# Eight one-bank accumulator tiles for the layers, and first scores issued inside the branch

## The chip, the cores and the metric

The kernel runs on one core of a Trainium2 chip. The metric is the device time of one execution in microseconds. Before the change it is 552.09 us, the median of 3 runs (551.27 to 553.7).

## What is computed

The program chains three parts, all in float32.

- Attention: 2 batches of 12 heads, 448 tokens, head width 64. Scores are q·kᵀ/8, capped as 30·tanh(s/30), then softmax, then times v. The heads are laid side by side, which gives x with 896 tokens and 768 columns.
- Layer 1: h = x·w_in (768 by 2048), g = max(h,0) + alpha·min(h,0), y = g·w_out (2048 by 768).
- Layer 2: the same shapes, with g = max(h,0)².

```python
x = attn_out.transpose(0, 2, 1, 3).reshape(B * S, H * D)
h = x @ w_in;  g = np.maximum(h, 0.0) + alpha * np.minimum(h, 0.0);  x = g @ w_out
h = x @ w_in2; r = np.maximum(h, 0.0); out = (r * r) @ w_out2
```

## The kernel before

**Start.** `start` (from line 448) issues the DMAs of the first k and q, eight warm-up matmuls into a pool of its own that is closed at once, and then the first three score products (`self.early`, line 474). After them it works out |cap| and reads it into a register of every engine (line 484). `attention_moe_moe` branches on that value (`tc.If`, line 855 on); `run(True)` is the branch that is taken here. In it SyncE and GpSimd begin with `constants` (alpha) and the loads of k, q and v.

**PSUM.** It has eight banks of 512 floats per partition. `start` makes a pool "ps" that lives to the end of the program: three tiles of two banks, `self.ps[n]` of shape [128, 2, 512]. `banks()` hands them out in turn: score products use both banks of a tile. A second pool in the attention has one two-bank tile, "pv".

**Attention** (`fast_attention`, 0 to 100 us): six steps in an order written out by hand for TensorE, ScalarE and VectorE. ScalarE does tanh and exp, TensorE scores and values. At its end three chains of layer 1 are already made (`up_now`).

**Layers** (`layers`, 100 to 546 us). A float32 product is three float32r matmuls: high·high, high·low, low·high, 448 columns each. So `multiply` (line 206) issues three matmuls for each 128 by 128 block of weights. An "up" stage makes, for each of 16 column blocks f, two chains of 18 matmuls, one per batch b, each into one bank. ScalarE and VectorE take a bank out: in layer 2 ScalarE writes max(h,0) (line 288) and VectorE multiplies it with max(h,0) again out of the bank (line 302); for some of the chains lines 296 and 297 do the same. A "down" stage forms a two by two block product by seven products P1 to P7 in place of eight; three banks at a time accumulate, are copied while they go on accumulating (`keep`, line 357), or are added to (lines 347, 348, 360).

The layers' work is not issued in program order. `Plan.order` simulates the engines with fixed costs and writes down, for each engine, the order in which it begins its operations; the instructions are then issued in just that order. A chain of "up" or "down" gets a bank when its first product is placed: the first of a list of free banks. A bank comes back to the end of that list when its last reader is done. The list begins with the two banks of a pool "hm" (which lie where "pv" was), then the first banks of the three "ps" tiles, then their second banks:

```python
banks = [hm.tile([P, self.S], F32, name=f"hm{n}", padded_shape=[P, 512]) for n in range(2)]
banks += [self.ps[n][:, e, :self.S] for e in range(2) for n in range(3)]
plan.tag("ps", banks)
```

Weights come as 64-bit words in 768 KB loads (`load`, line 231) into two raw buffers, each of which is free for the next load when VectorE has joined its words (line 245). In between lie ScalarE (line 247, for half of the second-stage loads also line 241) and VectorE (lines 249 to 254). Sixteen joined weights can wait. `split` makes high and low parts (lines 271 to 273).

The framework adds the semaphore waits: an instruction waits for the earlier instructions that it finds to touch the same tile.

Of the kernel before, what the change touches and what calls it, by code (L numbers as in the profile page):

```python
# [8 lines left out]
F32 = mybir.dt.float32  # L9
# [6 lines left out]
PSUM = bass.MemoryType.PSUM  # L16

P = 128
# [134 lines left out]
class Net:  # L153
# [294 lines left out]
    def start(self, ctx):  # L448

        nc, D, S = self.nc, self.D, self.S  # L450
        self.const = const = self.pool(ctx, "const", 1)
        self.cap_t = const.tile([P, 1], F32, name="cap_t")
        nc.scalar.dma_start(self.cap_t, self.cap.to_broadcast([P, 1]))
        self.raw = const.tile([P, 2, self.NC, P], I64, name="raw")
        x = const.tile([P, 2, self.B, self.NC, S], F32R, name="x")
        self.xh, self.xl = ([x[:, n, b] for b in range(self.B)] for n in range(2))

        first = self.raw[:, 1].bitcast(F32).rearrange("p n f -> p (n f)")
        k, q = (first[:, n * S:n * S + S] for n in range(2))
        nc.sync.dma_start(k, self.kT[:, 0])  # L460
        nc.sync.dma_start(q, self.qT[:, 0])
        self.kq = {0: (k, q)}
        self.ones = const.tile([P, P // 4], F32, name="ones")
        nc.gpsimd.memset(self.ones, 1.0)
        pool = self.pool(ctx, "ps", 1, space=PSUM)
        self.ps = [pool.tile([P, 2, 512], F32, name=f"ps{n}") for n in range(3)]
        self.nbank = -1
        idle = self.xh[0].rearrange("p c s -> p (c s)").bitcast(mybir.dt.bfloat16)[:, :P + 512]
        nc.gpsimd.memset(idle, 0.0)
        with self.tc.tile_pool(name="warm", bufs=1, space=PSUM) as pool:  # L470
            warm = pool.tile([P, 512], F32, name="warm")
            for _ in range(WARM):
                nc.tensor.matmul(warm, idle[:, :P], idle[:, P:], start=True, stop=True)
        self.early = [self.product(0, c) for c in range(3)]
        size = const.tile([P, 1], F32, name="size")
        nc.vector.tensor_scalar_mul(size, self.cap_t, -1.0)
        nc.vector.tensor_max(size, self.cap_t, size)
        self.guard_t = const.tile([P, 1], F32, name="guard_t")
        nc.scalar.activation(self.guard_t, size, AF.Exp, scale=-1.0)
        self.scale_t = const.tile([P, 1], F32, name="scale_t")  # L480
        nc.vector.reciprocal(self.scale_t, self.cap_t)
        nc.vector.tensor_scalar_mul(self.scale_t, self.scale_t, 1.0 / float(D) ** 0.5)
        nc.vector.tensor_scalar_mul(self.guard_t, self.guard_t, 1e-9)
        return nc.values_load(size.bitcast(I32)[0:1, :], skip_runtime_bounds_check_because="it is only compared")
# [275 lines left out]
    def run(self, fast):  # L760
        self.raws = []
        with ExitStack() as ctx:
            wp = self.pool(ctx, "wp", 1)
            splits = {t: [wp.tile([P, self.NC, P], F32R, name=f"{t}{n}") for n in range(SLOTS[t])] for t in ("wh", "wl")}
            self.wh, self.wl = splits["wh"], splits["wl"]
            self.early_g = [wp.tile([P, self.S], F32, name=f"early{f}") for f in range(AHEAD)]
            self.early_t = wp.tile([P, self.S], F32, name="t")
            self.constants()
            region = ExitStack()
            with ExitStack() as actx:  # L770
                self.ap = self.pool(actx, "ap", 2)
                self.early_w = [self.ap.tile([P, self.NC, P], F32, tag="ww", name="ww", bufs=AHEAD) for _ in range(AHEAD)]
                self.dp = self.pool(actx, "dp", 2, space=bass.MemoryType.DRAM)
                self.mm = self.pool(actx, "mm", 1, space=PSUM)
                if fast:
                    region = ctx.enter_context(ExitStack())
                    engines = {mybir.EngineType.PE, mybir.EngineType.Activation, mybir.EngineType.DVE}
                    region.enter_context(self.tc.manual_schedule(engines=engines))
                    self.fast_attention()
                else:  # L780
                    self.general_attention()
                    for f in range(AHEAD):
                        self.fetch(f)
                        self.advance(f, range(6))
                        self.up_now(f)
            lp = self.pool(ctx, "lp", 1, reuse_waits="tile")
            hm = self.pool(ctx, "hm", 1, space=PSUM, reuse_waits="tile")
            self.plan = plan = Plan()
            plan.tag("raw", [self.raw[:, (AHEAD + n) % 2] for n in range(2)])
            plan.tag("w", [lp.tile([P, self.NC, P], F32, name=f"w{n}") for n in range(SLOTS["w"])])  # L790
            for t in ("wh", "wl"):
                plan.tag(t, splits[t][AHEAD:])
            plan.tag("t", [self.early_t])
            plan.tag("g", [lp.tile([P, self.S], F32, name=f"g{n}") for n in range(SLOTS["g"])])
            for t in ("xh", "xl"):
                plan.tag(t, [lp.tile([P, self.S], F32R, name=f"{t}{n}") for n in range(SLOTS[t])])
            banks = [hm.tile([P, self.S], F32, name=f"hm{n}", padded_shape=[P, 512]) for n in range(2)]
            banks += [self.ps[n][:, e, :self.S] for e in range(2) for n in range(3)]
            plan.tag("ps", banks)
            self.layers()  # L800


# [62 lines left out]
```

## Time and profile before

| | us |
|---|---|
| median of 3 runs | 552.09 |
| the profiled execution, whole | 555.1 |
| its span, first to last instruction | 553.2 |
| attention | 0 to about 100 |
| layer 1 up, down | 100 to 208, 208 to 302 |
| layer 2 up, down | 317.6 to 441, 441 to 546 |

| engine | busy us | share of the span |
|---|---|---|
| TensorE matmuls | 531.8 | 96% |
| VectorE | 455.3 | 82% |
| ScalarE | 342.9 | 62% |

The profile is of one execution. TensorE's weight loads have a row of their own (PEld); a load runs beside the matmul before it. "Idle" is the time that an engine stood before an instruction, with the instruction that ended the wait. The trace gives a tile's name without its number, so "ps" is any of the six banks of the three pair tiles and "hm" any of the other two. Matmuls are pipelined and their ends are modelled, so lost time is counted here from start to start.

### The profile page before, as it was taken

To read this page: it belongs to the slowest core of one execution; us is meant where nothing else is said; L and a number is where in the kernel's file an instruction comes from. 1 tells how busy PE (TensorE), PEld (TensorE's weight loads), DVE (VectorE), ACT (ScalarE), POOL (GpSimd) and SP (SyncE) were. 2 spreads that over 40 slices of the span, in tenths; PEclk is the share of its full clock that TensorE was granted. 3 is DMA by queue.
4 is the path that set the end of the run, shared out by engine and by line. 5 is a ranking of instruction groups with operands and counts; after the bars stand their busy time and mean duration, and the time that the engine had idled before them with its cause. 6 is when DMAs were issued, how large, how long until landed. Compare 5 with 4: busy or idle time off the path is not lost.

```text
span 553.2 us, 7040 instructions
## 1 busy us (share of the span) xinstructions
PE 531.8 (96%) x2604; PEld 429.5 (78%) x2604; DVE 455.3 (82%) x639; ACT 342.9 (62%) x468; POOL 23.1 (4%) x36
## 2 busy tenths in 40 slices
PE   7889999999999999999999999999999999999995
PEld 2223345989898998798898887889788898999994
DVE  1799999698789889999998987869788799976661
ACT  6999992455567768956666543446655575455550
POOL 1000000000000000052000000000000000600000
PEclk9999999999999999999999999999999999999999
DMA  6445532145544555597003445645535400930111
GB/s 195 186 164 186 149 121 58 57 140 199 176 124 162 171 172 170 173 224 137 0 2 114 148 139 171 187 156 172 172 114 172 152 20 6 199 96 1 51 50 56
DMA packets 23034, 71.07 MB, mean 128 GB/s; under 512 B 4304, under 2 KB 13008, under 8 KB 22992
## 3 DMA queue, kind: packets, MB, share of 16 engines
q1 hardware_dynamic: 19392, 63.72, 35.3%
q0 software_dynamic: 3456, 6.82, 6.8%
q8 instruction: 22, 0.36, 0.3%
q14 instruction: 20, 0.16, 0.1%
q10 hardware_dynamic: 144, 0.00, 0.0%
HBM read 60.89 MB, written 2.79 MB: 115 GB/s over the span
## 4 chain that ended last, share of the span: by engine, by line
PE 41%; DVE 5%; ACT 3%; issue 1%; DMA 1%; DVEq 0%; ACTq 0%
PE ps L206 31%; PE hm L206 10%; DVE g L302 1%; ACT raw L241 1%; DMA raw<-in_w 1%; DVE w L245 1%; ACT w L247 1%; DVE raw L254 0%; ACT g L288 0%; DVE xl L273 0%; ACT wh L271 0%; DVE g L360 0%; DVE wl L272 0%; DVE raw L252 0%; DVE wl L273 0%
## 5 line engine op out<-in xcount | busy, mean ns | idle before, releaser
L206 PE MATMUL ps<-x,wh 128*128 128x448 f32 x576 | 166.9, 370 | 4.8 <-DVE g L302 2.4
L206 PEld LDWEIGHTS ps<-x,wh 128*128 128x128 f32 x576 | 106.0, 188 | 23.5 <-DVE g L302 6.1
L206 PE MATMUL ps<-x,wl 128*128 128x448 f32 x288 | 105.0, 365 | 0.5 <-DVE wl L273 0.5
L206 PE MATMUL ps<-xh,wh 128*128 128x448 f32 x256 | 94.9, 371 | 2.5 <-ACT g L357 1.4
L206 PE MATMUL ps<-xl,wh 128*128 128x448 f32 x256 | 94.1, 367 | 0.7 <-DVE xl L273 0.6
L206 PE MATMUL ps<-xh,wl 128*128 128x448 f32 x256 | 93.8, 367 | 0.0
L271 ACT CAST xh<-g 128x448 fp32r<-128x448 f32 x90 | 51.0, 568 | 56.6 <-PE ps L206 41.9
L271 ACT CAST wh<-w 128x768 fp32r<-128x768 f32 x77 | 64.5, 837 | 29.7 <-PE ps L206 20.7
L273 DVE TENSOR_TENSOR wl<-w,wh 128x768 fp32r<-128x768 f32 x77 | 73.3, 952 | 10.3 <-ACT wh L271 9.2
L273 DVE TENSOR_TENSOR xl<-g,xh 128x448 fp32r<-128x448 f32 x90 | 55.2, 618 | 15.5 <-ACT xh L271 15.2
L245 DVE SCALAR_TENSOR_TENSOR w<-w,raw 128x768 int32<-128x768 int32 x61 | 58.1, 954 | 11.9 <-ACT raw L241 11.3
L247 ACT ACTIVATE w<-raw 128x768 f32<-128x768 f32 x61 | 55.7, 913 | 18.2 <-DMA raw<-in_w 17.9
L206 PEld LDWEIGHTS ps<-x,wl 128*128 128x128 f32 x288 | 54.0, 187 | 5.3 <-DVE wl L273 0.9
L206 PEld LDWEIGHTS ps<-xh,wh 128*128 128x128 f32 x256 | 48.1, 188 | 10.5 <-ACT g L357 3.4
L206 PE MATMUL hm<-x,wh 128*128 128x448 f32 x192 | 54.5, 365 | 0.0
L206 PEld LDWEIGHTS ps<-xl,wh 128*128 128x128 f32 x256 | 48.1, 188 | 5.7 <-DVE xl L273 1.6
L206 PEld LDWEIGHTS ps<-xh,wl 128*128 128x128 f32 x256 | 48.1, 188 | 4.3
L254 DVE SCALAR_TENSOR_TENSOR raw<-raw 128x768 int32<-128x768 int32 x45 | 42.9, 956 | 1.0
L518 ACT ACTIVATE E<-ps,scale_t 128x896 f32<-128x896 f32 x42 | 40.2, 1025 | 3.3 <-PE ps L503 3.0
L206 PEld LDWEIGHTS hm<-x,wh 128*128 128x128 f32 x192 | 36.0, 187 | 2.9
L523 ACT ACTIVATE E<-E,cap_t 128x1792 f32<-128x1792 f32 (+1 forms) x24 | 38.2, 1623 | 0.0
L503 PE MATMUL ps<-q,k 64*128 64x448 f32 x132 | 30.4, 570 | 5.3 <-ACT E L518 3.0
(105 smaller groups left out, 672.9 us busy)
## 6 DMA issues: line engine op xcount, KB each, us to landing
raw<-in_w SPq DMA_DIRECT2D x64, 768.0 KB, 4.2
g<-g POOLq DMA_DIRECT2D x16, 224.0 KB, 5.2
w<-w POOLq DMA_DIRECT2D x8, 384.0 KB, 6.2
out_T<-g SPq DMA_DIRECT2D x12, 224.0 KB, 2.0
k<-in_kT SPq DMA_DIRECT2D x11, 224.0 KB, 5.0
q<-in_qT SPq DMA_DIRECT2D x11, 224.0 KB, 5.2
v<-in_vT SPq DMA_DIRECT2D x6, 384.0 KB, 5.5
rb<-row SPq DMA_DIRECT2D x10, 224.0 KB, 3.8
```

Source lines behind the costliest of these rows:

```text
L206: self.nc.tensor.matmul(ps, a[:, c, :], m, start=first and n == 0 and not more, stop=last and n == 2, skip_group_check=more)
L241: nc.scalar.mul(halves[:, :, :, 1], parts()[1].bitcast(F32), sign * 2.0 ** -60)
L245: nc.vector.scalar_tensor_tensor(bits, bits, 3, parts()[0], op0=ALU.logical_shift_left, op1=ALU.bitwise_or)
L247: plan.op("ACT", self.act(n) + 0.06, lambda: nc.scalar.mul(w.tile, parts()[1].bitcast(F32), 2.0 ** -112), [high, raw], [w])
L254: plan.op("DVE", self.dve(n), lambda: nc.vector.scalar_tensor_tensor(parts()[0], parts()[0], 29, parts()[1], op0=ALU.logical_shift_right, ...
L271: plan.op("ACT", self.act(n), lambda: nc.scalar.mul(h.tile, w.tile, -1.0) if sign < 0 else nc.scalar.copy(h.tile, w.tile), [w], [h])
L273: if sign < 0 else nc.vector.tensor_sub(l.tile, w.tile, h.tile.bitcast(F32)), [w, h], [l], port=True)
L302: plan.op("DVE", self.dve(S) + 0.06, lambda: nc.vector.scalar_tensor_tensor(g.tile, ps.tile, 0.0, g.tile, op0=ALU.max, op1=ALU.mult), [g, ...
L503: nc.tensor.matmul(ps[:, e, :], k[rows, c * P:c * P + P], q[rows], start=True, stop=True)
L518: nc.scalar.activation(es[-1][:, n % 2], ps, AF.Tanh, scale=self.scale_t)
L523: self.nc.scalar.activation(x, x, AF.Exp, scale=self.cap_t)
```

## The change

The "ps" pool moves from `start` into `run`, in the scope that ends with the attention. The first three score products move with it, behind the branch and ahead of `constants`; they are issued only where the fast attention runs. The layers no longer use the halves of the pair tiles: the pool "hm", opened after the attention's pools are closed, now has eight tiles of one bank. They are listed in an order that gives the same banks in the same sequence as before (6 and 7, where "pv" was, then 0, 2, 4, then 1, 3, 5), so `Plan.order` writes the same order of operations on the same banks.

```diff
@@ start
-        pool = self.pool(ctx, "ps", 1, space=PSUM)
-        self.ps = [pool.tile([P, 2, 512], F32, name=f"ps{n}") for n in range(3)]
-        self.nbank = -1
...
-        self.early = [self.product(0, c) for c in range(3)]
@@ run
-            self.constants()
             region = ExitStack()
             with ExitStack() as actx:
+                pool = self.pool(actx, "ps", 1, space=PSUM)
+                self.ps = [pool.tile([P, 2, 512], F32, name=f"ps{n}") for n in range(3)]
+                self.nbank = -1
+                self.early = [self.product(0, c) for c in range(3)] if fast else []
+                self.constants()
                 self.ap = self.pool(actx, "ap", 2)
...
-            banks = [hm.tile([P, self.S], F32, name=f"hm{n}", padded_shape=[P, 512]) for n in range(2)]
-            banks += [self.ps[n][:, e, :self.S] for e in range(2) for n in range(3)]
-            plan.tag("ps", banks)
+            banks = [hm.tile([P, self.S], F32, name=f"hm{n}", padded_shape=[P, 512]) for n in range(8)]
+            plan.tag("ps", [banks[n] for n in (6, 7, 0, 2, 4, 1, 3, 5)])
```

## Rows read from the trace of the kernel before

**Rows 1.** Page, part 1: busy us, share of the span, instructions.

```profile
PE 531.8 (96%) x2604; PEld 429.5 (78%) x2604; DVE 455.3 (82%) x639; ACT 342.9 (62%) x468; POOL 23.1 (4%) x36
```

**Rows 2.** Windows by stage: length, busy us (instructions) per engine, clock, DMA share, GB/s.

```profile
113.00:208.00 95.00, 95.00 (x464) 86.42 (x464) 81.97 (x113) 61.74 (x93) 0.00 (x0) 1.00 0.51 166
208.00:233.00 25.00, 23.66 (x112) 20.00 (x111) 24.97 (x39) 21.87 (x33) 0.00 (x0) 1.00 0.56 169
233.00:300.00 67.00, 66.27 (x321) 59.60 (x320) 64.10 (x100) 42.00 (x68) 10.62 (x12) 1.00 0.44 106
...
317.60:441.00 123.40, 118.67 (x563) 103.97 (x564) 97.97 (x136) 64.37 (x85) 0.00 (x0) 1.00 0.49 159
```

**Rows 3.** Timeline, 325.2 to 329: start, length, instruction, idle before and its end.

```profile
326.15 0.55 ACT L288 ACTIVATE g<-ps 128x448 f32<-128x448 f32 x1
...
326.36 0.36 PE L206 MATMUL ps<-x,wl 128*128 128x448 f32 x1
...
326.75 0.30 PEld L206 LDWEIGHTS ps<-x,wh 128*128 128x128 f32 x2 [0.41 <-ACT g L288]
...
327.27 0.36 PE L206 MATMUL ps<-x,wl 128*128 128x448 f32 x1
...
327.74 0.62 DVE L302 SCALAR_TENSOR_TENSOR g<-ps,g 128x448 f32<-128x448 f32 x1 [0.50 <-PE ps L206]
...
328.42 0.30 PEld L206 LDWEIGHTS ps<-x,wh 128*128 128x128 f32 x2 [0.56 <-DVE g L302]
```

**Rows 4.** Waits of weight loads, 317.6 to 441: total us, times, longest.

```profile
PEld ps L206 <- DVE g L302: 6.1, 10, 1.1
PEld ps L206 <- ACT g L288: 4.8, 8, 1.1
PEld ps L206 <- DVE g L297: 1.1, 2, 0.6
PEld ps L206 <- DVE x L348: 0.5, 1, 0.5
PEld ps L206 <- ACT g L296: 0.4, 1, 0.4
```

**Rows 5.** Windows inside layer 2 up, columns as in rows 2.

```profile
326.00:341.00 15.00, 13.86 (x63) 11.12 (x62) 10.75 (x15) 6.53 (x10) 0.00 (x0) 1.00 0.46 154
341.00:357.00 16.00, 16.00 (x82) 15.01 (x81) 13.94 (x19) 6.22 (x10) 0.00 (x0) 1.00 0.53 160
```

**Rows 6.** Chain that ended last: start, length, what, matmuls in an unbroken run.

```profile
285.87 14.88 PE ps L206 x72
...
352.84 5.40 PE ps L206 x27
```

**Rows 7.** Timeline, 456 to 459.5, columns as in rows 3.

```profile
457.25 0.53 ACT L357 COPY g<-ps 128x448 f32<-128x448 f32 x1 [0.69 <-PE ps L206]
...
458.14 0.54 ACT L357 COPY g<-ps 128x448 f32<-128x448 f32 x1
...
458.73 0.19 PEld L206 LDWEIGHTS ps<-xh,wh 128*128 128x128 f32 x1 [1.29 <-ACT g L357]
```

**Rows 8.** Timeline of the start, 0 to 40, columns as in rows 3.

```profile
5.00 0.44 PEld L503 LDWEIGHTS ps<-raw 64*128 64x128 f32 x4 [0.84 <-issue]
...
5.21 0.33 SPq L489 DMA_DIRECT2D slope_t<-in_alpha  x1
...
6.27 2.80 ACT L518 ACTIVATE E<-ps,scale_t 128x896 f32<-128x896 f32 x3 [1.49 <-PE ps L503]
```

**Rows 9.** Window of the attention's six steps, columns as in rows 2.

```profile
6.20:80.00 73.80, 68.43 (x388) 23.08 (x384) 61.11 (x74) 71.89 (x65) 0.40 (x2) 1.00 0.54 180
```

**Rows 10.** Loads of weights: six issues in a row from 369.38; all from 320 to 440.

```profile
369.38 21.22 SPq L231 DMA_DIRECT2D raw<-in_w  x6
...
raw<-in_w SPq DMA_DIRECT2D x25, 768.0 KB, 4.2
```

**Rows 11.** Page, part 3: code fetches, packets, MB, share of 16 engines' span.

```profile
q8 instruction: 22, 0.36, 0.3%
```

## The prediction

> **What bounds the kernel now.** I read the engine shares first, then one window per stage, then the waits inside the stage with the most unexplained time, and last its timeline. TensorE is busy 96% of the span [rows 1], so the question is what its few idle microseconds wait for. By stages [rows 2]: layer 1 up (113 to 208) has 464 matmuls in 95.00 us, all of them busy. From 208 to 233 VectorE is busy 24.97 of 25.00 us; it is the bound there. From 233 to 300 TensorE leads again. Layer 2 up (317.6 to 441) has 563 matmuls in 123.40 us, 0.219 each, though its work is layer 1 up's and VectorE is busy only 97.97 of 123.40 there. So layer 2 up loses time to waits, not to work.
>
> How much: in unbroken runs a matmul takes 5.40/27 = 0.200 us in this stage and 14.88/72 = 0.207 at 286 us [rows 6]. At 0.200, 563 matmuls are 112.6 us, so 10.8 of the 123.4 are lost. The weight loads' waits name the causes [rows 4]: lines 302, 288, 297 and 296 take a bank out, and they hold TensorE up 23 times, 12.4 us; one more (line 348) is the wait for the layer's input.
>
> The timeline shows the pattern [rows 3]. At 326.15 ScalarE begins to read one chain's bank. TensorE, which is in the middle of the other chain of the same f, stops when it would issue its next product, and goes on at 326.75, 0.05 after ScalarE's end (326.15 + 0.55). VectorE's line 302, which reads the first bank again and could start at 326.70, waits for TensorE's three matmuls and starts at 327.74. Then TensorE waits until line 302 has ended at 328.36 and goes on at 328.42. Neither needs the other's data. Which bank a chain has follows from `Plan.order`'s free list (its order alone, none of its times): in three of four consecutive f of this stage the two chains sit in the two halves of one pair tile, in the fourth in the two "hm" tiles. The windows agree [rows 5]: 326 to 341 has 63 matmuls in 15 us, while 341 to 357, in which the hm chains run, has 82 in 16 us, without a wait. In layer 1 up the two chains sit in two different tiles, and nothing waits [rows 2]. So the framework tracks the pair tile as one thing: a write into one half waits for a read of the other, and a read of the one for a write into the other.
>
> **The change part by part.** I count lost time from start to start. Around 326.75 three matmuls took 327.27 - 326.36 = 0.91 us and not 0.60, beside a weight-load wait of 0.41 [rows 3]: a wait costs its row less 0.10.
>
> (1) Layer 2 up. One tile per bank takes these 23 waits away. By the wait rows 12.4 - 2.3 = 10.1 us, by the count 10.8 less 0.4 for line 348's wait [rows 4], which is real and stays, 10.4. What is late next? With eight banks and two for each of 16 f, a bank comes round every four f, 4 x 123.4 / 16 = 31 us [rows 2], so no true bank wait follows. VectorE needs 97.97 of then 113 us [rows 2], 87%, and it loses its own half of the ping-pong too: 0.50 us of idle before line 302 [rows 3]. The raw loads: 25 are issued from 320 to 440, 4.8 us apart; the densest six came in 21.22 us, 4.24 apart [rows 10], so 25 need at least 106 us, and 120 - 10.4 = 109.6 remain. It fits, with little to spare. The pace is a second unknown: it is 0.200 in this stage and 0.207 in another [rows 6], and it changes after a wait, so without the waits the stage may run at either. At 0.207 throughout, 563 x 0.0067 = 3.8 us come back. Ends: 10.4 and 6.6. I take the middle, 8.5.
>
> (2) Layer 1 down, from 233. 321 matmuls at 0.203 (between the two paces) are 65.2 of 67.00 us: 1.8 lost; at 0.207 it would be 0.6 [rows 2]. The waits there are of the same kind, copies and additions on the other half. I take 1.4; ends 0.6 and 1.8. From 208 to 233 I take nothing: VectorE's idle time there is 0.03 us [rows 2], so TensorE can't gain more.
>
> (3) Layer 2 down. At 458.73 TensorE has waited for the copy of the other half, 458.14 + 0.54 = 458.68; its own bank's copy ended at 457.25 + 0.53 = 457.78 [rows 7]. That wait becomes 0.9 shorter. Ends 0.5, where the weights are late instead, and 0.9.
>
> (4) First scores behind the branch. No other instruction moves on TensorE, and the products issue no DMA. SyncE's first instruction behind the branch is alpha's load at 5.21, and the first score's weight load stood at 5.00 [rows 8]. TensorE has to read the same register, branch and wait for k and q before it issues, so I put its first score at about 5.4, 0.4 later. Ahead of SyncE's 5.21 it can't be: not under 0.2. The upper end is one code fetch more: 22 fetches hold 0.3% of 16 engines' span, 0.003 x 553.2 x 16 / 22 = 1.2 us each [rows 11], together 1.6. Nothing covers it: the first tanh waits for that product (1.49 us, at 6.27) [rows 8], and ScalarE is busy 71.89 of the next 73.80 us [rows 9], so attention ends later by the same amount. Queued behind the first scores on TensorE are the next products, which wait for tanh to empty a pair; constants' DMA and its GpSimd multiplication need nothing of TensorE. For the order that `Plan.order` writes, nothing changes, and so nothing for SyncE's and GpSimd's queues in the layers.
>
> (5) The seam. The new tiles lie over the attention's, so each one's first matmul waits for the last use of what lay there. The last readers of a pair tile there are two of ScalarE's out of `up_now`'s bank, and the layers' first two chains, 36 matmuls or 36 x 0.207 = 7.5 us [rows 6], go into the "pv" banks, as now. Behind them I cost the wait at nothing; if the first chain had to wait for those two reads it would be 2 x 0.55 = 1.1 us (line 288's length, [rows 3]).
>
> Sum: -8.5 - 1.4 - 0.9 + 0.4 = -10.4 us. Of the profiled execution (555.1 us, of which the span is 553.2) that leaves 544.7. The median of the runs is 3.0 lower, so the forecast for it is 552.1 - 10.4 = **541.7 us**. With every end on the good side -1.8 - 10.4 - 0.9 + 0.2 = -12.9, and about 1 us more if layer 2 down keeps the faster pace: 538. With every end on the bad side -0.6 - 6.6 - 0.5 + 1.6 = -6.1: 546.
>
> **The rivals.** *The loads take over in layer 2 up.* Both raw buffers are always in flight, and each load needs VectorE and ScalarE in their fixed order. If a load keeps 4.7 us (now 4.8, at best 4.24 [rows 10]), 25 take 117.5 us and part (1) gives 2.5 in place of 8.5: 547.7 us. For it: VectorE would wait for line 241 where it now waits for TensorE. Against it: much of the present 4.8 is VectorE waiting for TensorE inside a load's chain.
>
> *The waits stay.* If the framework already told the banks of a pair apart and the waits had another cause, only part (4) is left: 552.5 us. Against it: restarts 0.05 us after the read of the other half, again and again, and none where hm is used.
>
> [...]
>
> *The branch costs a fetch.* GpSimd and SyncE start behind the branch without a gap (5.21 [rows 8]), but TensorE's first instruction there is not seen now. A fetch of 1.2 us [rows 11] plus the wait for a transfer to land, 4.2 as for a load [rows 10], would put the first score up to 5 us later: 546.7. [...]
>
> **How the numbers follow.** Forecast (538 to 546) 77%, loads 12%, waits stay 5%, fetch 4%, clock 2%. The range holds the first, and the loads' and the fetch's times: 537.5 to 548. What a measurement of this kernel can tell from no change is about 0.5%, 2.8 us: 549.3 and 554.9 are the bounds. Forecast, loads and fetch lie below, 0.93 together; one in a hundred is left for a mixture that ends within, so faster 0.92, same 0.06, slower 0.02.
>
> **What would show it.** Right: in layer 2 up no weight load waits for lines 288, 296, 297, 302, line 302 starts at once behind line 288, and 563 matmuls take about 114 to 115 us; 458.73's wait is some 0.4 on its row; the first tanh is at about 6.7. Wrong: such waits for a bank still there (waits stay); waits of matmuls for line 273's high and low parts, with VectorE before line 245 waiting for line 241 (loads); a clock under 1 in a stage (clock); a first score past 6 (fetch). It is also wrong if TensorE's waits vanish but the stage's matmuls take 0.207 each: then part (1) was mis-sized by the pace.

## The result, and the profile after

The changed kernel takes 537.06 us (median of 4 runs, 536.3 to 540.72), the kernel before in the same runs 552.89 (4 runs, 551.27 to 554.69): 15.8 us less. The ratio is 0.9729, interval 0.9681 to 0.9777, with a fifth run of 538.62 in it; the two medians alone give 0.9714. Run once more on another occasion it took 537.17 (5 runs), ratio 0.9699 (0.9675 to 0.9724). The forecast was 541.7 with a range down to 537.5. Direction and mechanism were right; the gain was half as large again as forecast, and the median lies 0.4 us below the low end.

The profiled execution is the slowest of the four, 540.72 us; its span is 538.8, 14.4 less than before's 553.2. First the engine shares, as in [rows 1]:

```profile
PE 524.6 (97%) x2604; PEld 432.3 (80%) x2604; DVE 453.2 (84%) x639; ACT 343.5 (64%) x468; POOL 23.0 (4%) x36
```

The instruction counts are those of before. The windows answer to [rows 2] and [rows 5], the last three shifted by what this kernel is ahead there:

```profile
113.00:208.00 95.00, 94.79 (x459) 85.79 (x460) 82.87 (x115) 61.96 (x93) 0.00 (x0) 1.00 0.52 166
208.00:233.00 25.00, 24.75 (x118) 21.44 (x116) 24.48 (x38) 21.00 (x33) 0.00 (x0) 1.00 0.53 162
233.00:300.00 67.00, 66.42 (x328) 61.58 (x329) 65.93 (x104) 44.23 (x72) 10.62 (x12) 1.00 0.44 109
315.30:427.90 112.60, 112.57 (x564) 105.64 (x564) 95.99 (x136) 64.72 (x85) 0.00 (x0) 1.00 0.53 174
323.70:338.70 15.00, 15.00 (x77) 14.08 (x76) 12.88 (x18) 7.64 (x12) 0.00 (x0) 1.00 0.54 170
338.70:354.70 16.00, 16.00 (x82) 15.02 (x81) 13.34 (x18) 6.75 (x11) 0.00 (x0) 1.00 0.61 199
```

Layer 2 up is the change: from its first matmul to the first of the next stage it takes 112.7 us, where before it took 123.5. The stretch that had 63 matmuls in 15 us now has 77; its neighbour, which had no waits before, still has 82 in 16.

The timeline of the same f as in [rows 3] shows what stopped:

```profile
323.85 0.54 ACT L288 ACTIVATE g<-hm 128x448 f32<-128x448 f32 x1
...
324.05 0.36 PE L206 MATMUL hm<-x,wl 128*128 128x448 f32 x1
324.05 0.39 PEld L206 LDWEIGHTS hm<-x,wh 128*128 128x128 f32 x2
324.25 0.56 PE L206 MATMUL hm<-x,wh 128*128 128x448 f32 x2
...
324.85 0.62 DVE L302 SCALAR_TENSOR_TENSOR g<-hm,g 128x448 f32<-128x448 f32 x1
```

TensorE goes on every 0.20 us while ScalarE (line 288) and then VectorE (line 302) read the other chain's bank, and line 302 begins 1.00 us after line 288, not 1.59 as before. What weight loads still wait for in all the layers (100 to 545; total us, times, longest) is short. None of lines 288, 296, 297 and 302 is left of [rows 4]:

```profile
PEld hm L206 <- ACT g L357: 1.2, 3, 0.5
PEld hm L206 <- DVE xl L273: 1.0, 1, 1.0
PEld hm L206 <- DVE wl L273: 0.9, 1, 0.9
PEld hm L206 <- DVE x L348: 0.4, 1, 0.4
```

The chain that ended last has three unbroken runs of matmuls where [rows 6] had many short ones:

```profile
113.21 109.60 PE hm L206 x529
...
233.58 81.74 PE hm L206 x402
315.34 216.92 PE hm L206 x1067
```

Length by count gives means of 0.2072, 0.2033 and 0.2033 us. Start to start, the steady step is 0.207 us in layer 1 up, 0.203 in layer 1 down and 0.200 in layer 2 up. In layer 2 down it is 0.207, then 0.203, and 0.207 again from 445 us on.

The place of [rows 7], now some 14 us earlier:

```profile
444.34 0.36 PE L206 MATMUL hm<-xh,wl 128*128 128x448 f32 x1
444.54 0.36 PE L206 MATMUL hm<-xh,wh 128*128 128x448 f32 x1
444.61 0.53 ACT L357 COPY g<-hm 128x448 f32<-128x448 f32 x1
...
445.19 0.19 PEld L206 LDWEIGHTS hm<-xh,wh 128*128 128x128 f32 x1 [0.25 <-ACT g L357]
```

The product that began at 458.73 begins here at 444.54, 0.20 after the one before and ahead of the copy that it had waited for. The wait of 0.25 us at 445.19 ends behind that copy (444.61 + 0.53); with one-bank tiles it is a wait for the product's own bank.

The start, as in [rows 8]:

```profile
5.21 0.33 SPq L485 DMA_DIRECT2D slope_t<-in_alpha  x1
...
5.52 0.54 PEld L499 LDWEIGHTS ps<-raw 64*128 64x128 f32 x4 [1.35 <-issue]
...
6.43 0.32 PEld L499 LDWEIGHTS ps<-raw 64*128 64x128 f32 x2 [0.37 <-issue]
...
6.92 0.21 PEld L499 LDWEIGHTS ps<-raw 64*128 64x128 f32 x2 [0.17 <-issue]
...
7.21 1.01 ACT L514 ACTIVATE E<-ps,scale_t 128x896 f32<-128x896 f32 x1 [2.42 <-PE ps L499]
```

The first score's weights are loaded 0.52 later than before, the first tanh begins 0.94 later.

**The sum over the profiled pair.** I set the start of each of the 2604 matmuls against that of the same matmul before (positive: later). Behind the first scores +0.9 to +1.0; at 205 us +1.7; at 247 us +0.90; after layer 1 down (305 us) -2.2; before layer 2 up -2.3; after it -13.1; at the product of 458.73 -14.2; at the last matmul -13.6; at the end of the span -14.4. The 0.6 between the last product named and the last matmul is lost to pace: from 445 us on this execution steps by 0.207, where before stepped by 0.203 until 488. Waits between matmuls of the layers (steps of more than 0.22 us from 100 us on, each less the pace around it) sum to 18.3 us before and 2.8 after.

### The profile page after: what moved, and what is told of

Read it like the earlier page. It is cut to its first block, busy times and chain, and to the rows that moved or that the text cites. A ratio compares the mean times of both kernels' runs of the same rounds, so it can differ in the third digit from the quotient of the medians.

```text
span 538.8 us, 7022 instructions
## 1 busy us (share of the span) xinstructions
PE 524.6 (97%) x2604; PEld 432.3 (80%) x2604; DVE 453.2 (84%) x639; ACT 343.5 (64%) x468; POOL 23.0 (4%) x36
## 4 chain that ended last, share of the span: by engine, by line
PE 86%; DVE 5%; ACT 4%; DMA 2%; issue 1%; SPq 0%; POOL 0%; DVEq 0%; ACTq 0%; POOLq 0%
PE hm L206 77%; PE pv L549 3%; PE ps L206 2%; PE ps L499 2%; ACT E L514 2%; ACT E L519 1%; DVE s L535 1%; DMA r<-rows 1%; DMA k<-in_kT 1%; PE warm L470 1%; PE ps L568 0%; PE pv L559 0%; DVE raw L191 0%; DVE ww L193 0%; DVE raw L254 0%
## 5 line engine op out<-in xcount | busy, mean ns | idle before, releaser
L206 PE MATMUL hm<-x,wh 128*128 128x448 f32 x732 | 208.2, 365 | 0.0
L206 PEld LDWEIGHTS hm<-x,wh 128*128 128x128 f32 x732 | 137.1, 187 | 12.1 <-DVE x L348 0.4
L206 PE MATMUL hm<-x,wl 128*128 128x448 f32 x366 | 133.6, 365 | 0.5 <-DVE wl L273 0.5
L206 PE MATMUL hm<-xl,wh 128*128 128x448 f32 x336 | 123.3, 367 | 0.6 <-DVE xl L273 0.6
L206 PE MATMUL hm<-xh,wh 128*128 128x448 f32 x336 | 123.5, 368 | 0.2
L206 PE MATMUL hm<-xh,wl 128*128 128x448 f32 x336 | 123.2, 367 | 0.0
L206 PEld LDWEIGHTS hm<-x,wl 128*128 128x128 f32 x366 | 68.6, 187 | 6.6 <-DVE wl L273 0.9
L206 PEld LDWEIGHTS hm<-xh,wh 128*128 128x128 f32 x336 | 63.1, 188 | 6.8 <-ACT g L357 1.2
L206 PEld LDWEIGHTS hm<-xl,wh 128*128 128x128 f32 x336 | 63.1, 188 | 6.8 <-DVE xl L273 1.0
L206 PEld LDWEIGHTS hm<-xh,wl 128*128 128x128 f32 x336 | 63.1, 188 | 5.7
```

The costliest lines, as they stand in the source:

```text
L206: self.nc.tensor.matmul(ps, a[:, c, :], m, start=first and n == 0 and not more, stop=last and n == 2, skip_group_check=more)
```

## The experiments

**1. The first scores alone.** The kernel before, with only the pool of pairs and the first scores moved behind the branch. The layers keep the halves, and the pool lives to the end.

```diff
@@ start
-        pool = self.pool(ctx, "ps", 1, space=PSUM)
-        self.ps = [pool.tile([P, 2, 512], F32, name=f"ps{n}") for n in range(3)]
-        self.nbank = -1
-        self.early = [self.product(0, c) for c in range(3)]
@@ run
+            pool = self.pool(ctx, "ps", 1, space=PSUM)
+            self.ps = [pool.tile([P, 2, 512], F32, name=f"ps{n}") for n in range(3)]
+            self.nbank = -1
+            self.early = [self.product(0, c) for c in range(3)] if fast else []
```

> The kernel before with one part of the change alone: the pool of the three pair tiles and the first three score products stand in the branch, and the layers still use the halves of the pairs. Theory (the layers' gain comes from the waits between the halves alone, the moved scores cost what the trace after shows): the first tanh starts at 7.2 us instead of 6.27, every later matmul of the attention is 0.95 us later, layer 2 up still takes 123.4 us, the layers' weight loads still wait for lines 288 and 302 some 23 times there, and the time is the one of before plus about 1 us: 553.9 if before is 552.9 (ratio 1.002). Rival (the gain comes from where the scores and the pool stand, not from the tiles): a clear part of the 15.8 us is gained, ratio 0.99 or less.

Measured: 554.28 us against 552.19, ratio 1.0047 (1.0027 to 1.0067). The waits of weight loads in the layers are those of before:

```profile
PEld ps L206 <- DVE g L302: 6.0, 10, 1.1
PEld ps L206 <- ACT g L288: 5.1, 8, 1.1
```

So this part gains nothing and costs 1.5 to 3.7 us by the times, more than the expected 1. Its start, read as above, shows less than was expected: the weights come at 5.53, the first tanh at 6.68 and not at 7.2, 0.41 later than before, and the matmuls of the attention are 0.4 to 0.6 late, not 0.95:

```profile
5.53 0.33 PEld L499 LDWEIGHTS ps<-raw 64*128 64x128 f32 x4 [1.37 <-issue]
...
6.01 0.22 PEld L499 LDWEIGHTS ps<-raw 64*128 64x128 f32 x2 [0.15 <-issue]
...
6.68 1.91 ACT L514 ACTIVATE E<-ps,scale_t 128x896 f32<-128x896 f32 x2 [1.88 <-PE ps L499]
```

**2. Pair tiles in the new pool.** The changed kernel, with six of the eight banks as three tiles of two banks again. Pool, scope and bank order stay.

```diff
-            banks = [hm.tile([P, self.S], F32, name=f"hm{n}", padded_shape=[P, 512]) for n in range(8)]
+            pairs = [hm.tile([P, 2, 512], F32, name=f"hp{n}") for n in range(3)]
+            banks = [t[:, e, :self.S] for t in pairs for e in range(2)]
+            banks += [hm.tile([P, self.S], F32, name=f"hm{n}", padded_shape=[P, 512]) for n in range(2)]
```

> The kernel after, with the layers' banks 0 to 5 made as three tiles of two banks in the layers' own pool, and 6 and 7 as two tiles of one bank; the banks, their list and the order of the operations are the same. Theory (a wait is drawn between the two banks of one tile): the 18.4 us of waits between layer matmuls come back, where after has 2.8, layer 2 up takes 123 us again, and the time is that of before plus the 0.95 us of the later first scores: 553.8 against 552.9 (ratio 1.002). Rival (what matters is that the attention's pool ends and the layers have a pool of their own): the time of after stays, 537 (ratio 0.971).

Measured: 553.68 us, ratio 1.0025 (1.0011 to 1.0038), and the waits are back, now on tile "hp":

```profile
PEld hp L206 <- DVE g L302: 6.1, 10, 1.1
PEld hp L206 <- ACT g L288: 4.2, 8, 0.8
...
PEld hp L206 <- DVE g L297: 1.1, 2, 0.6
```

This is the decisive one. The banks and their order are those of the changed kernel; only what counts as one tile differs. Where the pool ends and where the first scores stand have no part in the gain; what the framework takes as one tile makes all of it.

**3. Four pairs.** As 2, with the last two banks made one pair too.

```diff
-            pairs = [hm.tile([P, 2, 512], F32, name=f"hp{n}") for n in range(3)]
+            pairs = [hm.tile([P, 2, 512], F32, name=f"hp{n}") for n in range(4)]
             banks = [t[:, e, :self.S] for t in pairs for e in range(2)]
-            banks += [hm.tile([P, self.S], F32, name=f"hm{n}", padded_shape=[P, 512]) for n in range(2)]
```

> As three_pairs, but banks 6 and 7 are also the halves of one tile: four tiles of two banks. The suspected cost is doubled at the place that had none. Theory: the first two chains and, in layer 2 up, every fourth f (the one whose two chains had the two hm tiles) now have the waits too, in the layer 1 up stage as well. Laying the order of the operations over the times of after, waits between halves would come to 18.7 us for the three pairs and 28.8 for four, and three pairs lose 15.6 us in truth; so four lose about 24, 8 more than three: about 562 us (ratio 1.016), with the stretch that has no waits in before (341 to 357) now at about 63 to 70 matmuls in 16 us instead of 80. Rival: 537 (ratio 0.971).

Measured: 559.69 us, ratio 1.0134 (1.0116 to 1.0152). One pair more lengthens the kernel by another 6.0 us, and the waits grow with it (line 302 from 10 to 14, line 288 from 8 to 14). The direction is the expected one, the size is not: 6.0 us and not 8, and the stretch that had no waits in before takes 16.8 us for 80 matmuls where it took 16.0, which is 76 in 16 us and not 63 to 70. Of the 7.3 us of new waits 2.2 are in layer 2 up, the rest in the other stages:

```profile
PEld hp L206 <- DVE g L302: 8.1, 14, 1.1
PEld hp L206 <- ACT g L288: 6.0, 14, 0.6
```

**4. Another order of the free list.** The kernel before, its pairs untouched; only the list's first order differs, so that the two chains of one f share a pair less often.

```diff
-            plan.tag("ps", banks)
+            plan.tag("ps", [banks[n] for n in (3, 4, 2, 0, 5, 1, 6, 7)])
```

> The kernel before with nothing but another order in the list of free banks: pair 1 first half, pair 2 first half, pair 0 first half, hm0, pair 0 second half, hm1, pair 1 second half, pair 2 second half. The order of the operations is the same, every tile is as before; only which two chains share a pair differs. Theory: in layer 2 up the two chains of one f no longer sit in one pair, so their waits go, but other chains share pairs now; laid over the times of after, the waits between halves come to 10.6 us where the list of before has 18.7. So some 43% of the 15.6 us are saved: about 546 us (ratio 0.988). Rival (the waits have nothing to do with which chains share a tile): the time of before, 552.9 (ratio 1.000). Rival (one-bank tiles save something else as well, for every chain): no gain here either.

Measured: 546.96 us, ratio 0.9891 (0.9863 to 0.9918). One reordered list gives a third of the gain by the medians, two fifths by the ratios, without a new tile. Layer 2 up has no wait left, and line 302, the longest holder in [rows 4], is gone. The waits on lines 288 and 290 are now in layer 1 up, which waits 7.1 us where it waited 0.3:

```profile
PEld ps L206 <- ACT g L288: 4.5, 8, 0.7
PEld ps L206 <- ACT t L290: 4.2, 9, 0.8
```

Without a wait, layer 2 up still takes 116.3 us here and not 112.7, because it steps by 0.207, as its unbroken runs show:

```profile
342.65 11.16 PE ps L206 x54
```

**The kernels side by side.** Counted as in the sum above, in one profile of each, the waits between layer matmuls come to 2.8 us in the changed kernel, 11.9 with the other list, 18.3 before, 18.2 with three pairs, 19.1 with the first scores alone and 25.5 with four pairs. The median times are 537.1, 547.0, 552.2, 553.7, 554.3 and 559.7 us. Less its waits, each median lies between 533.9 and 535.5.

**5. The changed kernel again, and two edits of its start.** The first is unedited, a measure for the other two.

> The changed kernel once more, as the measure for the two kernels beside it. Its ratio against the kernel before should be 0.973 again (537 us beside 552), and its first tanh should begin 0.3 to 1.0 us after before's 6.27; in four other kernels this start differed by 0.7 us from one profiled execution to the next.

Measured: 537.17 us against 553.32, ratio 0.9699 (0.9675 to 0.9724). Its start:

```profile
5.51 0.45 PEld L499 LDWEIGHTS ps<-raw 64*128 64x128 f32 x4 [1.35 <-issue]
...
6.14 0.21 PEld L499 LDWEIGHTS ps<-raw 64*128 64x128 f32 x2 [0.17 <-issue]
...
6.80 1.91 ACT L514 ACTIVATE E<-ps,scale_t 128x896 f32<-128x896 f32 x2 [2.02 <-PE ps L499]
```

The weights come at 5.51 as in the first profile, the tanh 0.41 earlier than there. So 0.52 of the 0.94 is the branch, and 0.42 differs between executions of the same code.

The second issues the first two products and their tanh ahead of the branch, out of a pool that is closed there. A tile of the constants, "early_all", holds their result, and the attention's pool waits by tile.

```diff
@@ start
+        with self.tc.tile_pool(name="first", bufs=1, space=PSUM) as pool:
+            self.ps = [pool.tile([P, 2, 512], F32, name=f"first{n}") for n in range(2)]
+            self.nbank = -1
...
+            for c in range(2):
+                nc.scalar.activation(self.first[:, c], self.product(0, c), AF.Tanh, scale=self.scale_t)
@@ run
...
-                self.early = [self.product(0, c) for c in range(3)] if fast else []
...
```

> The changed kernel, with the first two score products and their tanh issued ahead of the branch again (in a pool of two pair tiles that is closed there; the other products stay in the branch). Theory: the move behind the branch costs 0.4 to 0.95 us, paid in full because ScalarE is without a gap from the first tanh on. Then the first tanh is back at 6.3 to 6.9 and the time is 0.1 to 0.2% below the changed kernel's: 536 to 536.6 us, which would beat both. Rival: the start is covered somewhere on the way (VectorE's stretch at 208, the loads) or is lost in what differs from one execution to the next: the same time as the changed kernel within 0.1%. A second rival: the first use of the new pool's tiles behind the branch waits for the early tanh, and the second tanh comes later: 0.1 to 0.3% above.

Measured: 537.63 us, ratio 0.971 (0.9684 to 0.9737), not to be told from 537.17. The first weights are loaded early again, at 5.13, but the tanh is at 7.04 and not at the expected 6.3 to 6.9; and near 55 us this profile loses 1.6 us more, where VectorE waits for a transfer and a product for VectorE:

```profile
5.13 0.51 PEld L506 LDWEIGHTS first<-raw 64*128 64x128 f32 x4 [0.96 <-PE warm L470]
...
6.04 0.34 PEld L506 LDWEIGHTS first<-raw 64*128 64x128 f32 x2 [0.41 <-issue]
...
6.79 0.28 PEld L506 LDWEIGHTS first<-raw 64*128 64x128 f32 x2 [0.41 <-issue]
...
54.25 0.23 DVE L592 TENSOR_SCALAR r<-r,guard_t 128x14 f32<-128x14 f32 x1 [1.52 <-DMA r<-rows]
```

The gain expected of it didn't come. That wait is not its own: in the first profile of the changed kernel VectorE waits 0.7 us for the same transfer, in four_pairs 1.0, in the others it doesn't appear.

The third has nine warm-up matmuls for eight, which shortens TensorE's idle time ahead of its first product: the first weight load waits 0.98 us and not 1.35.

```diff
-WARM = 8
+WARM = 9
```

> The changed kernel with nine warm-up matmuls in place of eight, which shortens TensorE's idle time before the branch by one warm-up matmul. In the changed kernel's profile the second matmul of the first product comes 0.87 us after the first, in before's 0.62. If that is the idle gap's doing, it is 0.62 here and the first tanh about 0.25 us earlier (6.9 to 7.0), which the time can hardly show (0.05%). If the gap has nothing to do with it, 0.87 stays and the first tanh is at 7.2 or, should the ninth matmul delay the branch, later.

Measured: 538.14 us, ratio 0.9717 (0.9692 to 0.9742), again not to be told apart. The weight loads stay 0.91 apart (the second half of the expectation), so that much less idle time doesn't make the first product faster:

```profile
5.57 0.53 PEld L499 LDWEIGHTS ps<-raw 64*128 64x128 f32 x4 [0.98 <-issue]
...
6.48 0.27 PEld L499 LDWEIGHTS ps<-raw 64*128 64x128 f32 x2 [0.38 <-issue]
```

The length of the gap alone doesn't decide it either: before and other_list both begin at 5.00 after a wait of 0.84, and their second loads come at 5.63 and 5.91. Here is before's:

```profile
5.63 0.19 PEld L503 LDWEIGHTS ps<-raw 64*128 64x128 f32 x2 [0.19 <-issue]
```

None of the runs points to a version faster than the changed kernel.

## Why the prediction was right, and where its sizes were wrong

The mechanism is shown. Experiment 2 takes the one-bank tiles away and leaves the rest: the waits and the time return. Experiment 3 makes one pair more, experiment 4 changes which chains share a pair: the time follows the waits.

- **Part (1), layer 2 up: forecast 8.5, measured 10.8.** This is the step that failed in size. I had two paces, didn't know which one the stage would have, and took the middle of 6.6 and 10.4. It kept the faster one, 0.200 us from start to start, in all four profiles of the changed kernel and its edits. So the whole count came through. What decides the pace is open: in experiment 4 the same stage, just as free of waits, ran at 0.207 and gained 7.2 us. Two readings were wrong besides. [rows 4] holds 10 + 8 + 2 + 1 = 21 waits for a bank, not 23 (the wait rows then give 10.3 us and not 10.1, which the forecast didn't use). And line 348's 0.4 was not to be taken off: that wait ends at 317.65, where the stage's first counted matmul begins, so the count of 10.8 never held it.

- **What is late next: nothing, as chosen.** VectorE is busy 95.99 of 112.60 us, 85%. The loads, which I feared might hold at 4.7 to 4.8 us each, went faster. VectorE's waits for TensorE at line 302, 7.5 us in this stage before, are gone; that this is what sped the loads up is argued, not shown. The 25 issues now run from 319.7 to 427.1, 107.4/24 = 4.48 us apart:

```profile
L231 SPq DMA_DIRECT2D raw<-in_w x25: 327/328/328, 319.7 to 427.1; - x25
```

- **Part (2), layer 1 down: forecast 1.4, ends 0.6 and 1.8; measured 3.1.** Three pieces, from the matmul starts of before: waits inside the window 1.8; two more at 300.8 and 301.8 us, just behind the window's end at 300, 0.76; and before ran at 0.207 from 269 to 300, now at 0.203, 0.5. I had cut the window at a round number and then let one pace stand for the stage.
- **From 208 to 233: nothing, as forecast.** TensorE goes out of it 0.90 late, though it came in 1.7 late (before had run its last 28 us of layer 1 up at 0.200 per matmul, here it was 0.207): VectorE, busy 24.48 of 25.00 us, sets that stretch.
- **Part (3): forecast 0.9, measured 1.1.** The product of 458.73 now follows the one before without a wait.
- **Part (4), the branch: forecast 0.4, measured 0.52 to the first weights** in the changed kernel, inside 0.2 to 1.6, and not covered, as said. The tanh's 0.94 holds 0.42 that belongs to the execution. The times of experiments 1 and 2 say more (2.1 and 1.5 us at the medians), and nothing in their traces shows the rest. The edit that issues the first products ahead of the branch didn't give it back. What makes up the difference stays open, and since the first tanh of before's own code came at 6.27 and 6.97 in two profiles, no pair of profiles can size it at the tanh.
- **Part (5), the seam: nothing, as forecast.** The matmuls stay 0.9 to 1.1 late through 113 us without a new wait.
- **Not foreseen:** the stretch from the last matmul to the end took 6.48 us before and 5.72 now, but 6.19 when the same kernel ran again; over all profiles it lies between 5.7 and 6.7. I count it as scatter.

With every end on the good side I had 538, and 537.06 is still below it. Part (1) reached its best end in full and a little more (10.4 forecast, 10.8 measured), and part (2)'s end was too tight. These sizes are of one pair of executions, 14.4 us apart, where the medians are 15.8 apart.

**The rivals.** *Loads:* 4.48 us each, refuted, though VectorE's waits for line 241 ahead of line 245 did grow in layer 2 up, 6.8 to 7.8 us, the sign named for this rival. *Waits stay:* refuted by the waits after and by experiment 2. *Clock* (2% in the forecast): in the changed kernel it reads 1.00 in every window from 0 to 532.6 us, through 1067 matmuls in one piece, and its mean over a run is 0.996 to 1.000 in all runs here. What a lower one would cost, no run shows. *Fetch:* refuted by the first weights at 5.52, behind SyncE's first instruction at 5.21 by 0.31; code fetches are 22 with 0.36 MB as before.

## What to carry to other kernels

Where a framework derives waits from tiles, make each tile as large as what one engine writes while another reads, and no larger: two ping-pong accumulators in one tile are not ping-pong. The sign in a profile is an engine that restarts 0.05 us after a read of data that it doesn't need, in some rounds and not in others of the same work. When such waits go, count them from start to start over the whole stage, with the pace of that stage in that execution, and look at who else was waiting on the other side.

## What the runs showed of the hardware

**The layers' matmuls have several steady paces.** The same stage with the same instructions runs for tens of us at 0.200, 0.203 or 0.207 us per matmul of 448 columns, each with its own weight load (2604 of each in a profile). Most changes come at a wait (before goes from 0.207 to 0.200 at 179.9 us, behind a step of 0.31), but not all: in the first profile of the changed kernel the step goes from 0.200 to 0.207 where layer 2 down begins, and to 0.203 near 431 us, with no step over 0.21 us in between. In four profiles of the changed kernel and its two edits, 400 steps of layer 1 up took 82.67 us three times and 80.00 once (nine_warm), and the last 424 steps of layer 2 down took 87.6 once and 85.9 three times. The two rows below are the stretch of layer 2 from the changed kernel's second profile and from nine_warm, and answer to 216.92 above:

```profile
314.48 215.25 PE hm L206 x1067
```

```profile
312.89 215.25 PE hm L206 x1067
```

Layer 1 up's 2.7 and layer 2 down's 1.7 us together are 4.4, about as much as the runs of one kernel differ (536.3 to 540.72). Which pace comes when is open.

**The first product can run at half its later pace while the clock column says 1.00.** Weight loads of score products follow each other 0.37 to 0.38 us apart later on. At the start the step was 0.91, then 0.75, twice the later one, in other_list, whose start is before's own code:

```profile
5.00 0.51 PEld L503 LDWEIGHTS ps<-raw 64*128 64x128 f32 x4 [0.84 <-issue]
...
5.91 0.34 PEld L503 LDWEIGHTS ps<-raw 64*128 64x128 f32 x2 [0.41 <-issue]
...
6.66 0.34 PEld L503 LDWEIGHTS ps<-raw 64*128 64x128 f32 x2 [0.41 <-issue]
...
6.97 1.91 ACT L518 ACTIVATE E<-ps,scale_t 128x896 f32<-128x896 f32 x2 [2.21 <-PE ps L503]
```

Ahead of it TensorE does nothing but its warm-up matmuls, 0.43 us apart for 512 columns; 512 / 0.43 is 1.2 columns per ns, where a layer matmul at 0.200 us passes 448 / 0.200 = 2.2. The step falls to 0.37 at a moment that differs between executions, from about 5.6 us (before) to 7.2 (other_list), and moves the first tanh of one and the same code by up to 0.7 us (6.27 and 6.97). The granted clock reads 1.00 in every window of the start (0 to 8 us, nine profiles). So an edit of the start that is worth less than 0.7 us can't be judged from one pair of profiles.
